# Longformer attention, then a gated MLP, on one core: key and query loads of 80 rows, and another order of the opening

## The chip, the core and the metric

One core of a Trainium2 chip runs the kernel. The time is the device time of one execution in microseconds (us); the times given are medians over runs. TensorE (PE in the profile) does the matmuls and transposes, VectorE (DVE) and ScalarE (ACT) the elementwise work, GpSimd (POOL) small copies and the loads that cast from fp32 to fp16 on their way, SyncE (SP) issues the other transfers. Each engine works through its own instructions in the order of the program; semaphores hold an instruction until what it needs is there.

## The reference

Attention with a band of 32 keys to either side and eight global positions (rows and columns), over 8 batches of 8 heads, 576 positions and 64 channels. Its output, laid out as 4608 tokens of 512 channels, goes through an MLP.

```python
scores = scale * np.matmul(q, k.transpose(0, 1, 3, 2))
mask = np.abs(pos[:, None] - pos[None, :]) <= 32
mask = mask | is_global[:, None] | is_global[None, :]
scores = np.where(mask, scores, -1000000000.0)
...
x = np.matmul(attn, v)            # [8, 8, 576, 64] -> [4608, 512]
h = x @ w_in                      # w_in [512, 2048]
out = (h * np.cos(h)) @ w_out     # w_out [2048, 512]
```

## The kernel before

The 64 heads are handled as 32 pairs; a half-batch is two pairs (four heads). A pair goes through these units, named here as in the string `OPENING`, with the pair's number behind the letter:

- `k`, `q` (`local_k`, `local_q`, for the first ten pairs): sixteen transposes (L598) and sixteen 8-column matmuls that pick the global keys or queries (L319), all into one PSUM bank, which ScalarE or VectorE then copies out (L320, L607, L618, L619; which of the two is told by the strings `ENGINES`). From pair 10 on these are single copies on VectorE from tiles that a transposing DMA has filled (L610, L622).
- `s`: ten score matmuls (L634), exponentials on ScalarE (L637, L641), the mask on VectorE (L638, L642). From pair 10 on L705 to L709.
- `p`: twenty matmuls with the values (L649), then reciprocals and the product `xn` on VectorE (L669).
- `x`: five transposes (L686) and copies into `xT` (L687 to L692); `X` puts in the global rows of a whole batch, on GpSimd (L676).
- `1`: an mlp unit of the first matmul, four 128x512 matmuls (L767) with cosine (L773) and product (L774); it needs the tokens of its tile of 512 in `xT`. `2`: an mlp unit of the second, four matmuls (L805). There are 144 of each. Those that stand in no string are done at the end, alternating.

Other steps issue loads, nearly all from GpSimd's queue: `L` (L284) a half-batch's k and q in natural layout, one row of eight positions to a partition (72 rows, with 3 rows ahead for k and 4 more for q: `KP` is 75, `QP` 76), into `kn`, `qn` or `room`; `M` (L386) its values; `W` (L898) a quarter of `w_in`; `O` (L902) `w_out`; `E` and `A` (L342) gather the global rows; `K` (L271, L275) casts a half-batch from DRAM to DRAM, which `B` brings in on SyncE's queue. `C` (L400) casts the first values on GpSimd, `y` (L406) puts global values in, `I` (L949) loads eight registers on GpSimd. `H` and `g` handle the global rows, `Z` builds masks, `S` spreads global values (L412). `warm` before the string issues dense matmuls on a tile of ones (13, then 4 and 4); `f` (`fill`) would issue a given number of 128x184 matmuls of the same tile into a part of `pv` that nobody reads; it does not occur in the string of before.

The string is worked through step by step, and every step adds its instructions behind those already on each engine. From half-batch 6 on a fixed string per half-batch (`ORDER`) takes over.

```python
nc.gpsimd.dma_start(dst[s % NN][0:n, hs[0] : hs[1]].rearrange("x h r d -> x h (r d)"),
                    dview(src, base - lead * RW * D, (RW * D, n), (S * D, hs[1] - hs[0]), (1, RW * D)))
```

Of the kernel before, what the change touches and what calls it, by code (L numbers as in the profile page):

```python
# [10 lines left out]
FP16 = mybir.dt.float16  # L11
# [6 lines left out]
B, H, S, D = 8, 8, 576, 64  # L18
# [11 lines left out]
RW = 8  # L30
KS = 120
NK5 = 5
KPAD = 3
KP = KPAD + S // RW
QP = S // RW + 4
OFF = (0, 136, 488, 680, 328)
WID = (136, 192, 192, 192, 160)
CA, CB = 488, 384
# [10 lines left out]

SIXTH = "sa 2 2 2 2 sz pa 1 1 2 xa pz G 1 1 2 xz n 1 1 D0 2 kc qc D1 1 kd qd D2 2 1 T"  # L50

OPENING = ("s0 k1 q1 E2 k3 L2 L3 H2 I0 S4 k2 q2 C0.0 q3 C0.1 y0 s1 M1 k4 L4 p0 S5 s2 q4 q5 S2 p1 Z0 M2 s3 "
# [5 lines left out]
ENGINES = ("DAADAAAADD", "DAADADAAAA", "AAAADDDDAD", "AAAAAAAAAA")  # L58
WARM = 13
OK_ALL = float(P * (B * NP * 2 * BP + B))  # L60

# [1 line left out]
def view(ap, *dims):  # L63

    return bass.AP(ap.tensor, ap.offset, [ap.ap[0], *[list(d) for d in dims]])


def dview(ap, offset, *dims):

    return bass.AP(ap.tensor, ap.offset + offset, [list(d) for d in dims])  # L70
# [134 lines left out]
def kernel(  # L205
# [16 lines left out]
    keep = es.enter_context(tc.tile_pool(name="keep", bufs=1))  # L222
# [27 lines left out]
    NN = 4  # L250
    kT = [keep.tile([P, 2, KT], FP16, name=f"kT{i}") for i in range(2)]
    qT = [keep.tile([P, 2, QT], FP16, name=f"qT{i}") for i in range(2)]
    kn = [keep.tile([KP, 2 * 2, RW, D], FP16, name=f"kn{i}") for i in range(2)]
    qn = [keep.tile([QP, 2 * 2, RW, D], FP16, name=f"qn{i}") for i in range(2)]
    vn32 = work.tile([P, 8 * 512], FP32, tag="g", name="vn32")
    room = work.tile([P, NF, TT], FP16, tag="g", name="room")
    w_out16 = const.tile([P, NF, DM], FP16)
    for i in range(2):
        kn.append(room[0:KP, 8 * i : 8 * i + 4].rearrange("p h (r d) -> p h r d", d=D))
        qn.append(room[0:QP, 8 * i + 4 : 8 * i + 8].rearrange("p h (r d) -> p h r d", d=D))  # L260
    vw = [keep.tile([P, NB, 2, D + 1], FP16, name=f"vw{i}") for i in range(NV)]
    NK = 4
    kw = [keep.tile([P, NB, P], FP16, name=f"kw{i}") for i in range(NK)]
# [14 lines left out]
    def load_qk(s, hs=(0, 4)):  # L278

        base = (s * 4 + hs[0]) * S * D  # L280
        for src, dst, n, lead in ((k, kn, KP, KPAD), (q, qn, QP, 0)):
            if s == 0:
                dst, n, lead = [dst[0][lead:]], S // RW, 0
            nc.gpsimd.dma_start(dst[s % NN][0:n, hs[0] : hs[1]].rearrange("x h r d -> x h (r d)"),  # L284
                                dview(src, base - lead * RW * D, (RW * D, n), (S * D, hs[1] - hs[0]), (1, RW * D)))
# [28 lines left out]
    def pick_globals(pr, t, src, ones, n, to):  # L314

        h0 = 2 * (pr % 2)
        for r in range(RW):
            for h in range(2):
                nc.tensor.matmul(t[h * D : (h + 1) * D], src[:n, h0 + h, r], ones[:n, r], start=r == 0, stop=r == RW - 1, skip_group_check=True)  # L319
        COPY[ENGINES[3][pr]](to, view(t, (0, to.shape[1]), (1, G)))  # L320

# [6 lines left out]
    p8 = keep.tile([P, 1], FP32)  # L328
# [169 lines left out]
    def build_mask5():  # L498
# [17 lines left out]
        for t in (0, 1, 4, 2, 3):  # L516
            b0 = D if t == 0 else 0
            n = P if t == 0 else WID[t]
            nc.vector.tensor_scalar(mask5[:, OFF[t] : OFF[t] + n], band5[:, b0 : b0 + n], nk[:, t : t + 1], None, ALU.mult)
        for t in range(NK5):  # L520
            g0 = OFF[t] + (P if t == 0 else D)
            nc.vector.tensor_copy(mask5[:, g0 : g0 + G], view(val[:, t : t + 1], (0, G)))
# [49 lines left out]
    def k5(pr):  # L572
        return kw[pr % NK][:, 0:NK5]

    def q5(pr):
        return qb[pr % NK][:, 0 : 2 * NK5].rearrange("p (n t) c -> p n (t c)", t=2)
# [14 lines left out]
    def turned(src, pr, n):  # L591

        bank = ps.tile([P, 512], FP32, tag="h", bufs=2, name="bank")
        t = view(bank.bitcast(FP16), (QP, RW), (1, QP))
        h0 = 2 * (pr % 2)
        for r in range(RW):
            for h in range(2):
                nc.tensor.transpose(t[h * D : (h + 1) * D, r, 0:n], src[:n, h0 + h, r], ident16[:n, :n])  # L598
        return t, bank[:, 400 : 400 + G]

    def local_k(pr):
        to = kw[pr % NK][:, :, G:]
        if pr < 2 * HY:
            t, g = turned(kn[pr // 2 % NN], pr, KP)
            if pr < PK:
                pick_globals(pr, g, kn[pr // 2 % NN], one_k, KP, k5(pr)[:, :, 0:G])
            COPY[ENGINES[0][pr]](k5(pr)[:, :, G:].rearrange("p n (j r) -> p n j r", r=RW),  # L607
                           view(t, (KS // RW, NK5), (1, KS // RW), (QP, RW)))
        else:
            nc.vector.tensor_copy(to, view(kT[pr // 2 % 2][:, pr % 2], (QB, NB), (1, W)))  # L610

    def local_q(pr):
        to = qb[pr % NK][:, :, G:]
        if pr < 2 * HY:
            t, g = turned(qn[pr // 2 % NN], pr, QP)
            if pr < PK:
                pick_globals(pr, g, qn[pr // 2 % NN], one_q, QP, q5(pr)[:, 1:, 0:G])
            COPY[ENGINES[2][pr]](qb[pr % NK][:, 0, 0:G], t[:, :, 0])  # L618
            COPY[ENGINES[1][pr]](q5(pr)[:, :, G:].rearrange("p n (j r) -> p n j r", r=RW),  # L619
                           view(t[:, :, 1:], (KS // RW, NK5), (1, KS // RW), (QP, RW)))  # L620
# [3 lines left out]
    def scores5(pr):  # L624
# [4 lines left out]
        for t in (0, 1, 4, 2, 3):  # L629
            i, c = (0, OFF[t]) if OFF[t] < CA else (2, OFF[t] - CA)  # L630
            q0 = 0 if t == 0 else P * t - D
# [12 lines left out]
    def values5(pr):  # L644
# [3 lines left out]
        def add(h, t, c0, m, slot, p0, start, stop):  # L648
            nc.tensor.matmul(pv[p0 : p0 + m, h, X * slot : X * slot + X], pm[:, h * CN + OFF[t] + c0 : h * CN + OFF[t] + c0 + m], vp[:, t, h0 + h],  # L649
                             start=start, stop=stop, skip_group_check=True)  # L650
# [254 lines left out]
    with tc.manual_schedule():  # L905
# [6 lines left out]
        for t in (qn[0][64:QP, 2:4], kn[0][0:KPAD, 2:4]):  # L912
            nc.scalar.memzero(t.rearrange("p a b c -> p (a b c)"))
        load_qk(0, (0, 2))
        nc.gpsimd.iota(p_i, pattern=[[0, 1]], base=0, channel_multiplier=1)
        nc.gpsimd.iota(d5_i[:, 0:D], pattern=[[-1, D]], base=56, channel_multiplier=1)
# [3 lines left out]
        nc.gpsimd.affine_select(ident16, ident16, [[-1, P]], ALU.is_equal, 0.0, base=0, channel_multiplier=1)  # L920
        nc.gpsimd.iota(tok_i, pattern=[[1, RW]], base=0, channel_multiplier=RW)
        load_qk(0, (2, 4))
        nc.scalar.memzero(vn_of(0)[0:G, 1:].rearrange("p t d -> p (t d)"))
        nc.scalar.activation(x_sq[:, 0:1], pio2, AF.Exp)
# [3 lines left out]
        build_band()  # L928
        index_rows(1)
        load_qk(1)  # L930
        build_ones()
        build_mask5()
# [67 lines left out]
        outs_by[0] = NTT * NF  # L1000
        for step in OPENING.split():
            if step in "+-":
# [9 lines left out]
        for s in range(6, B * NP // 2):  # L1012
            for step in (SIXTH if s == 6 else ORDER).split():
# [15 lines left out]
                else:  # L1029
                    f, pr = (STEPS | OTHER)[step[0]], 2 * s + "azcd".index(step[1])  # L1030
# [54 lines left out]
```

## Time and profile before

| | |
|---|---|
| median of 3 runs | 356.44 us (356.26 to 356.76) |
| the profiled execution | 355.74 us |
| its span, first to last instruction | 354.0 us |
| mean granted TensorE clock | 0.943 |
| TensorE, VectorE, ScalarE, GpSimd busy | 337.8, 254.3, 223.7, 112.0 us |
| mlp matmuls L767 and L805 | 142.8 and 136.2 us, 381 and 379 ns each |

Of a page or table row: an instruction row gives start, length, engine, line, operation, `out<-in`, shape and count, and in brackets how long its engine had been idle just before and what released it. A stage row gives stretch, length, busy time and number of instructions of each engine, then the granted clock (1.00 is full), the share of the DMA engines and GB/s. A load row gives its size and the time from issue to landing.

### The profile page before, as it was taken

The page shows a single profiled execution, that of the slowest core. Times are in us where ns is not written, and L with a number is a line of the kernel's source. Part 1 is how long each engine was busy: PE and PEld are TensorE (multiplying, and loading weights), DVE is VectorE, ACT ScalarE, POOL GpSimd, SP SyncE. Part 2 cuts the span into 40 slices and gives each one's busy share as a digit, 9 for nine tenths or more (in the row PEclk, how much of TensorE's full clock was granted, in tenths as well). Part 3 has the DMA queues.
Part 4 walks back from the last instruction along what each step waited for, and adds up shares of the span by engine and source line. Part 5 has one row for each costly group of instructions (what it writes and reads, how often), then busy time and mean ns, then how long its engine had stood idle before and what let it go on. Part 6 is the DMA issues. An engine that isn't in the chain of part 4 may idle for free.

```text
span 354.0 us, 8610 instructions
## 1 busy us (share of the span) xinstructions
PE 337.8 (95%) x3294; PEld 177.5 (50%) x3294; DVE 254.3 (72%) x622; ACT 223.7 (63%) x411; POOL 112.0 (32%) x213
## 2 busy tenths in 40 slices
PE   7689999999899999999999999999999999999993
PEld 2468885545454444544444444454545444444442
DVE  6647768959997878787877879797968566556410
ACT  4446657696669685867777676767767756644300
POOL 8665593276802505150705070506000100000000
PEclk9955559999999999999999999999999999999998
DMA  6999999959999999999999999999980000100112
GB/s 105 160 135 81 161 161 200 171 61 149 179 149 118 157 182 144 192 125 185 134 178 142 166 126 206 138 180 142 175 100 32 30 31 30 59 31 31 58 64 68
DMA packets 170708, 43.68 MB, mean 123 GB/s; under 512 B 158468, under 2 KB 165812, under 8 KB 170484
## 3 DMA queue, kind: packets, MB, share of 16 engines
q0 software_dynamic: 73552, 18.64, 58.7%
q1 hardware_dynamic: 96118, 24.17, 48.0%
q8 instruction: 28, 0.46, 0.6%
q10 hardware_dynamic: 990, 0.25, 0.3%
q14 instruction: 20, 0.16, 0.2%
HBM read 44.74 MB, written 19.17 MB: 181 GB/s over the span
## 4 chain that ended last, share of the span: by engine, by line
PE 82%; DMA 7%; ACT 5%; issue 2%; POOL 1%; SPq 1%; DVE 1%; ACTq 0%; POOLq 0%
PE ph L767 32%; PE po L805 32%; DMA qn<-in_q_dram 4%; PE pv L649 3%; DMA kT<-k 3%; PE bank L598 2%; PE tx L750 2%; PE st L705 2%; ACT e L708 2%; PE st L634 2%; PE bank L319 2%; PE pv L725 1%; ACT e L713 1%; PE tx L686 1%; PE po L787 1%
## 5 line engine op out<-in xcount | busy, mean ns | idle before, releaser
L767 PE MATMUL ph<-xT,w_in 128*128 128x512 f16 x576 | 142.8, 381 | 0.8 <-DVE g L774 0.2
L805 PE MATMUL po<-w_out,g 128*128 128x512 f16 x560 | 136.2, 379 | 0.0
L773 ACT ACTIVATE cos<-ph 128x512 f16<-128x512 f32 x144 | 84.4, 597 | 69.7 <-PE ph L767 62.6
L774 DVE TENSOR_TENSOR g<-cos,ph 128x512 f16<-128x512 f16 x144 | 95.9, 684 | 40.9 <-ACT cos L773 39.4
L805 PEld LDWEIGHTS <-g 128*128 128x128 f16 x560 | 53.4, 98 | 63.4 <-issue 0.3
L767 PEld LDWEIGHTS <-w_in 128*128 128x128 f16 x576 | 53.9, 98 | 61.7 <-issue 4.8
L676 POOL COPY xT<-xg 128x4 f16 x64 | 18.9, 295 | 45.3 <-DVE xT L753 38.2
L708 ACT ACTIVATE e<-st 128x512 f16<-128x512 f32 x44 | 23.9, 594 | 11.0 <-PE st L705 10.9
L709 DVE TENSOR_TENSOR pm<-e,mask 128x512 f16<-128x512 f16 x44 | 18.7, 425 | 16.1 <-ACT e L708 14.7
L983 POOL COPY gate<-xn 1x1 f16<-1x1 f16 x8 | 1.4, 181 | 85.4 <-DVE xn L736 85.4
L275 POOL DMA_DIRECT2D q<-in_q_dram x11 | 24.3, 2212 | 0.0
L823 ACT ACTIVATE xn<-xn 128x1536 f16<-128x1536 f16 (+1 forms) x16 | 22.6, 1415 | 0.0
L736 DVE TENSOR_TENSOR xn<-pv,r_all 128x768 f16<-128x768 f32 x22 | 21.1, 958 | 1.0
L812 DVE COPY o<-po 128x512 f32<-128x512 f32 x18 | 12.4, 688 | 8.3 <-PE po L805 8.3
L275 POOL DMA_DIRECT2D k<-in_k_dram x11 | 18.2, 1653 | 0.6 <-issue 0.6
L386 POOL DMA_DIRECT2D vw<-in_v_dram x16 | 15.3, 1102 | 7.6 <-DVE pm L638 4.2
L810 ACT COPY o<-po 128x512 f32<-128x512 f32 x17 | 10.0, 585 | 12.2 <-PE po L805 12.1
L773 ACT ACT_TABLE_LOAD x13 | 16.7, 1283 | 0.2
L637 ACT ACTIVATE e<-st 128x488 f16<-128x488 f32 x20 | 10.5, 578 | 9.1 <-PE st L634 9.0
L610 DVE COPY kw<-kT 128x1320 f16<-128x1320 f16 x22 | 15.3, 694 | 0.1
L708 ACT ACT_TABLE_LOAD x11 | 14.1, 1283 | 0.2
L705 PEld LDWEIGHTS <-kw 64*128 64x128 f16 x484 | 8.3, 95 | 11.0 <-issue 6.8
(182 smaller groups left out, 394.7 us busy)
## 6 DMA issues: line engine op xcount, KB each, us to landing
out_dram<-o SPq DMA_DIRECT2D x35, 256.0 KB
vw<-v SPq DMA_DIRECT2D x32, 165.0 KB
v<-in_v_dram POOLq DMA_DIRECT2D x11, 288.0 KB, 5.4
k<-in_k_dram POOLq DMA_DIRECT2D x11, 288.0 KB, 8.3
q<-in_q_dram POOLq DMA_DIRECT2D x11, 288.0 KB, 11.0
w_in<-in_moe_w_in_dram POOLq DMA_DIRECT2D x4, 512.0 KB, 10.0
w_out<-in_moe_w_out_dram POOLq DMA_DIRECT2D x1, 2048.0 KB, 17.4
vw<-v SPq DMA_DIRECT2D x11, 135.0 KB
```

Of the source, the lines that this page charges most:

```text
L275: nc.gpsimd.dma_start(dst[s].rearrange("t (h d) -> t h d", h=4), dview(src, base, (D, S), (S * D, 4), (1, D)))
L386: nc.gpsimd.dma_start(vn16(s)[G:P, :, h, 0:D], dview(v, ((4 * s + h) * S - 24) * D, (D, KS), (KS * D, NK5), (1, D)))
L676: nc.gpsimd.tensor_copy(xT[:, :, bass.ds(pool_idx[g] + b * S, 1)], xg[:, :, g : g + 1])
L705: nc.tensor.matmul(st[j // 8 * 2 + h][:, j % 8 * C : j % 8 * C + C], kp[hp, j], qp[hp, j], start=True, stop=True)
L708: nc.scalar.activation(e[:, 0:512], st[h], AF.Exp, scale=scale)
L709: nc.vector.tensor_tensor(view(pm[:, h], (1, 512)), e[:, 0:512], view(mask, (1, 512)), ALU.mult)
L736: nc.vector.tensor_tensor(view(xn, (384, 2), (D, 6), (1, D)), view(pv, (512, 2), (65, 6), (1, D)), view(rp, (6, 2), (1, 6), (0, D)), ALU.mult)
L767: nc.tensor.matmul(ph, w_in16[:, j, f * P : (f + 1) * P], xT[:, j, t * TT : (t + 1) * TT], start=(j == 0), stop=(j == NC - 1))
L773: nc.scalar.activation(cos, ph, AF.Sin, bias=pi / 2.0)
L774: nc.vector.tensor_tensor(g, cos, ph, ALU.mult)
L805: nc.tensor.matmul(po, g16[:, f, s * P : (s + 1) * P], w_out16[:, f], start=(f == 0), stop=(f == NF - 1))
L823: nc.scalar.activation(view(xn, (BP * P, 2), (1, n)), view(xn, (BP * P, 2), (1, n)), AF.Square, accum_out=x_sq[:, s : s + 1])
```

## The change

`KQ`, 80, takes the place of `KP` and `QP` as the number of partitions of the tiles and rows that `L` loads for half-batches 1 to 4. The load of half-batch 0 (72 rows, in two halves) and all that reads the tiles are as before: the further rows are loaded and not used. The string `OPENING` and the four strings `ENGINES` are others.

```diff
+KQ = 80
...
-ENGINES = ("DAADAAAADD", "DAADADAAAA", "AAAADDDDAD", "AAAAAAAAAA")
+ENGINES = ("ADDADAAAAA", "AADAADAAAD", "DDADAADAAD", "ADAAAAAAAA")
...
-    kn = [keep.tile([KP, 2 * 2, RW, D], FP16, name=f"kn{i}") for i in range(2)]
-    qn = [keep.tile([QP, 2 * 2, RW, D], FP16, name=f"qn{i}") for i in range(2)]
+    kn = [keep.tile([KQ, 2 * 2, RW, D], FP16, name=f"kn{i}") for i in range(2)]
+    qn = [keep.tile([KQ, 2 * 2, RW, D], FP16, name=f"qn{i}") for i in range(2)]
...
-        for src, dst, n, lead in ((k, kn, KP, KPAD), (q, qn, QP, 0)):
+        for src, dst, n, lead in ((k, kn, KQ, KPAD), (q, qn, KQ, 0)):
```

The start of the old and of the new string:

```diff
-OPENING = ("s0 k1 q1 E2 k3 L2 L3 H2 I0 S4 k2 q2 C0.0 q3 C0.1 y0 s1 M1 k4 L4 p0 S5 s2 q4 q5 S2 p1 Z0 M2 s3 "
-           "S3 + k5 k7 p2 s5 q7 x0 W0 k6 p3 s4 W1 q9 S6 x2 x3 M3 q6 x1 p4 q8 S7 k8 W2 s7 k9 p5 s6 W3 "
-           "X0 O0 1 x4 1 : S8 1 K5 1 p6 M4 1 1 1 S9 n0 x5 1 p7 1 1 x6 1 Z1 E1 1 1 1 1 "
+OPENING = ("E0 q1 E2 k2 s0 q3 W0 k1 H2 q2 I0 L2 f2 L3 Z0 C0.1 C0.0 S7 y0 S2 S4 s1 S3 - M1 k3 p0 k4 s2 q5 "
+           "p1 Z1 s3 f4 L4 S6 k5 x0 q7 x1 q4 k6 M2 p2 S5 s4 W1 k7 p3 s5 q6 M3 k8 x3 p4 s6 k9 x2 + W2 "
+           "q8 O0 p5 X0 s7 q9 p6 s8 1 S9 1 1 1 n0 W3 : x4 p7 1 1 x6 1 + 1 1 S8 1 x5 n2 M4 "
```

The lines of the changed kernel are one higher from L36 on. TensorE between the dense matmuls on ones and s1, before; one row of each unit (here s0, k1, q1, k3 and k2, q2 and q3, y0, s1; `kn_87` and `qn_89` are half-batch 0, `kn_88` and `qn_90` half-batch 1):

```order
L634 MATMUL st<-qb_102,kw_98 128x136
...
L598 MATMUL bank<-ident_70,kn_87 64x75
...
L598 MATMUL bank<-ident_70,qn_89 64x76
...
L598 MATMUL bank<-ident_70,kn_88 64x75
...
L598 MATMUL bank<-ident_70,qn_90 64x76
...
L406 MATMUL rows<-vw_94,one_v 8x256
...
L634 MATMUL st<-qb_103,kw_99 128x136
```

The same place of the change (q1, k2, s0, q3, k1, q2, two fillers, y0, s1):

```order
L599 MATMUL bank<-ident_70,qn_89 64x76
...
L599 MATMUL bank<-ident_70,kn_88 64x75
...
L635 MATMUL st<-qb_102,kw_98 128x136
...
L599 MATMUL bank<-ident_70,qn_90 64x76
...
L599 MATMUL bank<-ident_70,kn_87 64x75
...
L599 MATMUL bank<-ident_70,qn_90 64x76
...
L497 MATMUL pv<-ones_114 128x184
...
L407 MATMUL rows<-vw_94,one_v 8x256
...
L635 MATMUL st<-qb_103,kw_99 128x136
```

s0 and k1 have moved behind units of half-batch 1, one unit (k3) has gone behind s1, and two fillers have come in.

GpSimd from the load of half-batch 1 to the cast of the first values, before:

```order
L284 DMA kn_88<-in_k_dram 75x4x512
L284 DMA qn_90<-in_q_dram 76x4x512
L342 DMA vg_108<-in_v_dram,gidx_rows 128x64 x2
L284 DMA room<-in_k_dram 75x4x512
L284 DMA room<-in_q_dram 76x4x512
...
L951 TENSOR_LOAD gidx_row
L951 ISA x16
L400 CAST vw_94<-vn_91 128x5x2x64 x2
```

and of the change:

```order
L285 DMA kn_88<-in_k_dram 80x4x512
L285 DMA qn_90<-in_q_dram 80x4x512
L343 DMA kg_107<-in_k_dram,gidx_rows 128x64 x2
L343 DMA vg_108<-in_v_dram,gidx_rows 128x64 x2
L899 DMA w_in_133<-in_moe_w_in_dram 128x4x512
...
L952 TENSOR_LOAD gidx_row
L952 ISA x16
L285 DMA room<-in_k_dram 80x4x512
L285 DMA room<-in_q_dram 80x4x512
...
L401 CAST vw_94<-vn_91 128x5x2x64 x2
```

Two gathers and the first quarter of `w_in` have come ahead of the registers, and the loads of half-batches 2 and 3 (`room`) have gone behind them, still ahead of the cast.

VectorE ahead of s10, where the first pairs of the other kind are made (`qb_104`, `kw_100` are pair 10, `qb_105`, `kw_101` pair 11), before:

```order
L967 MEMSET pv 64x2
L622 COPY qb_105<-qT_86 128x11x56
L774 TENSOR_TENSOR g<-cos,ph 128x512
L622 COPY qb_104<-qT_86 128x11x56
...
L610 COPY kw_100<-kT_84 128x11x120
...
L610 COPY kw_101<-kT_84 128x11x120
L709 TENSOR_TENSOR pm<-e,mask 128x512 x2
```

and of the change:

```order
L968 MEMSET pv 64x2
L623 COPY qb_105<-qT_86 128x11x56
L611 COPY kw_100<-kT_84 128x11x120
L611 COPY kw_101<-kT_84 128x11x120
L775 TENSOR_TENSOR g<-cos,ph 128x512 x2
L623 COPY qb_104<-qT_86 128x11x56
L775 TENSOR_TENSOR g<-cos,ph 128x512
L710 TENSOR_TENSOR pm<-e,mask 128x512 x2
```

Both key copies are now ahead of the query copy of pair 10. From s12 on TensorE's rows are the same in both, twelve rows (six fillers and their weight loads) later.

More of the change, by code (lines that the diff above doesn't have):

```diff
@@ L258 @@
     for i in range(2):
-        kn.append(room[0:KP, 8 * i : 8 * i + 4].rearrange("p h (r d) -> p h r d", d=D))
-        qn.append(room[0:QP, 8 * i + 4 : 8 * i + 8].rearrange("p h (r d) -> p h r d", d=D))
+        kn.append(room[0:KQ, 8 * i : 8 * i + 4].rearrange("p h (r d) -> p h r d", d=D))
+        qn.append(room[0:KQ, 8 * i + 4 : 8 * i + 8].rearrange("p h (r d) -> p h r d", d=D))
     vw = [keep.tile([P, NB, 2, D + 1], FP16, name=f"vw{i}") for i in range(NV)]
```

6 rows, old and new, of the table OPENING are left out of this document.

## The prediction

> **What bounds the kernel now.** The page first: span, busy time, and the granted clock in 40 slices of 8.85 us.
>
> ```profile
> span 354.0 us, 8610 instructions
> ...
> PE 337.8 (95%) x3294; PEld 177.5 (50%) x3294; DVE 254.3 (72%) x622; ACT 223.7 (63%) x411; POOL 112.0 (32%) x213
> ...
> PEclk9955559999999999999999999999999999999998
> ```
>
> TensorE is busy for 95% of the span, so the end moves with its work, its holes and its clock. The clock is at half in slices 3 to 6. In the table by stage a mean of 0.77 over 50 to 60 us says that it came back about 54.6 us, after 46% of that stage.
>
> ```profile
> 50.00:60.00 10.00, 10.00 (x86) 5.78 (x83) 8.02 (x21) 6.73 (x13) 6.36 (x6) 0.77 1.22 189
> ```
>
> The same table for two stretches around the fall, one around a hole much later, and the half-clock stretch as a whole (columns: stretch and length, then busy us and count of PE, PEld, DVE, ACT, POOL, then clock, DMA share, GB/s):
>
> ```profile
> 13.60:17.10 3.50, 1.23 (x65) 1.14 (x64) 1.81 (x4) 1.78 (x7) 1.01 (x3) 0.99 1.33 164
> 17.10:20.50 3.40, 1.20 (x37) 1.04 (x38) 0.23 (x1) 0.75 (x2) 2.77 (x4) 0.50 1.02 140
> ...
> 88.70:92.30 3.60, 1.96 (x12) 0.75 (x11) 3.60 (x6) 1.88 (x2) 3.60 (x4) 1.00 1.39 182
> 20.50:52.40 31.90, 31.50 (x636) 26.31 (x633) 21.80 (x67) 19.08 (x52) 20.27 (x30) 0.50 1.38 134
> ```
>
> The clock fell at 17.1 us (0.99, then 0.50). The stretch just before has TensorE busy for 1.23 of 3.50 us (35%); 1.96 of 3.60 us (54%) at 88.7 us did not bring the clock down. The level below which it falls, in these terms, lies between 35% and 54%. Once it is down, 31.50 of 31.90 us of small matmuls do not bring it back; the mlp matmuls behind 52.4 us do. So from 20.5 to 52.4 us **a half-clocked TensorE is the bound**, while VectorE is busy for 21.80 us (68%) and ScalarE for 19.08 us (60%). What made the holes is in TensorE's rows in order of time:
>
> ```profile
> 15.04 0.47 PE L598 MATMUL bank<-ident,kn 75*64 75x75 f16 x16 [1.44 <-DMA kn<-in_k_dram]
> ...
> 18.57 0.17 PE L319 MATMUL bank<-one_k,kn 75*64 75x8 f16 x1 [2.31 <-issue]
> 19.47 0.72 PE L598 MATMUL bank<-ident,qn 76*64 76x76 f16 x16 [0.73 <-DMA qn<-in_q_dram]
> ...
> 21.48 1.23 PE L406 MATMUL rows<-vw,one_v 128*8 128x256 f16 x5
> 22.63 0.91 PE L634 MATMUL st<-qb,kw 64*128 64x136 f16 x10
> ```
>
> A wait for the second keys (1.44 us), one that the profile gives to nothing (2.31 us), one for the second queries (0.73 us). From s1 at 22.63 us on, TensorE has hardly a hole. The next one of size comes at 92 us, where s10 waits behind the copy k10, which took 1.88 us on VectorE:
>
> ```profile
> 92.27 0.50 PE L705 MATMUL st<-qb,kw 64*128 64x64 f16 x22 [1.64 <-POOL kw L582]
> ```
>
> ```profile
> 90.29 1.88 DVE L610 COPY kw<-kT 128x1320 f16<-128x1320 f16 x1
> ```
>
> **The change, part by part.** The 80-row loads first. Two loads of 72 rows, then the two of the second half-batch (75 rows of k, 76 of q), with KB and us from issue to landing; behind them GpSimd's own rows:
>
> ```profile
> kn<-in_k_dram POOLq DMA_DIRECT2D x1, 144.0 KB, 7.8
> qn<-in_q_dram POOLq DMA_DIRECT2D x1, 144.0 KB, 7.9
> ```
>
> ```profile
> qn<-in_q_dram POOLq DMA_DIRECT2D x1, 304.0 KB, 13.1
> kn<-in_k_dram POOLq DMA_DIRECT2D x1, 300.0 KB, 9.4
> ```
>
> ```profile
> 4.93 0.68 POOL L284 DMA_DIRECT2D qn<-in_q_dram  x1
> 5.61 0.69 POOL L284 DMA_DIRECT2D kn<-in_k_dram  x1
> 6.29 1.15 POOL L284 DMA_DIRECT2D qn<-in_q_dram  x1
> 7.74 1.07 POOL L342 DMA_INDIRECT vg<-in_v_dram,gidx_rows  x1 [0.31 <-DVE one_v L503]
> ...
> 10.14 0.82 POOL L284 DMA_DIRECT2D room<-in_k_dram  x1
> ...
> 17.49 1.39 POOL L400 CAST vw<-vn 128x640 f16<-128x640 f32 x2 [2.88 <-issue]
> ```
>
> k landed at 5.61 + 9.4 = 15.0 us, q of nearly the same size, issued 0.68 us later, at 6.29 + 13.1 = 19.4 us, and its issue cost 0.46 us more. In the 72-row pair k and q took the same (7.8 and 7.9 us; q landed at 4.93 + 7.9 = 12.8 us). 76 rows, not the queue, make q late. With 80 rows I let q behave as k does: k itself took 15.0 - 12.8 = 2.2 us behind its forerunner, so q lands about 17 us (bounds: 15.0 with k, 19.4 as now), and three issues ahead of the value cast C0 save 1.4 us.
>
> [...]
>
> Now the order, to s1. The new one runs q1, k2, s0, q3, k1, q2, fill 2, y0, s1; the old one s0, k1, q1, k3, k2, q2, q3, y0, s1. So s0 and k1, which ran before 13 us, are kept back into the stretch that had 1.23 us, and the next has k1, q2 and the fill. GpSimd has two more gathers (about 2.4 us: the old pair started at 7.74 and the load behind it at 10.14), one more w_in issue (some 0.8 us, about what such an issue of a load takes here) and 1.4 us less of issues ahead of C0, which ended at 18.88 us: now about 20.7 us, so y0 can start there (21.48 us before) and s1 comes **about 0.6 us earlier**. k3 has been moved behind s1. Holes remain: ahead of q1, ahead of k2 until 15.0 us, about 16.3 to 17 us, perhaps the 2.31 us again, and ahead of y0. In the stretch from 13.6 us I count k2 0.65, s0 0.5, q3 and k1 up to 0.7: 1.2 to 1.9 us (35 to 54%); in the next one the rest of q3, k1, q2, 0.15 of fill: 1.4 to 2.1 us (41 to 62%). That is inside the gap between the two measured stretches, mostly in its upper half. **I take it that the clock stays up**, narrowly, and price both.
>
> From s1 to the first mlp unit the new order has, besides all that the old one has there, k3, s8, p6 and four fillers. Unit times at half and at full clock, each from a row's start to that of the next:
>
> ```profile
> 28.81 1.56 PE L649 MATMUL pv<-vw,pm 128*128 128x65 f16 x20
> 30.30 0.91 PE L634 MATMUL st<-qb,kw 64*128 64x136 f16 x10
> 31.14 0.72 PE L598 MATMUL bank<-ident,room 75*64 75x75 f16 x16
> ...
> 32.09 0.70 PE L598 MATMUL bank<-ident,room 75*64 75x75 f16 x16
> ...
> 52.38 1.89 PE L767 MATMUL ph<-xT,w_in 128*128 128x512 f16 x4
> 54.07 0.71 PE L686 MATMUL tx<-ident,xn 128*128 128x128 f16 x5
> 54.60 2.76 PE L767 MATMUL ph<-xT,w_in 128*128 128x512 f16 x12
> 57.20 1.03 PE L649 MATMUL pv<-vw,pm 128*128 128x65 f16 x20
> 58.16 2.76 PE L767 MATMUL ph<-xT,w_in 128*128 128x512 f16 x12
> ...
> 71.68 0.55 PE L634 MATMUL st<-qb,kw 64*128 64x136 f16 x10
> 72.16 1.90 PE L805 MATMUL po<-w_out,g 128*128 128x512 f16 x8
> ```
>
> Half clock: p 1.49, s 0.84, k 0.95 us, an mlp unit 1.69 us, a filler 184/512 of a quarter of that, 0.15 us. Full clock: p 0.96, s 0.48, an mlp unit 2.60/3 = 0.87 us. From s12 on both programs have the same matmuls in the same order, so what counts is the time at which that point is reached.
>
> Clock up. TensorE then needs little more than half of its time, and VectorE is next. Its rows:
>
> ```profile
> L638 DVE TENSOR_TENSOR pm<-e,qT 128x488 f16<-128x488 f16 x12 | 4.5, 403 | 0.2 <-ACT e L637 0.2
> L669 DVE TENSOR_TENSOR xn<-pv,r_all 128x640 f16<-128x640 f32 x5 | 4.1, 824 | 0.2
> L642 DVE TENSOR_TENSOR pm<-e,qT 128x768 f16<-128x768 f16 x6 | 3.3, 554 | 1.4 <-ACT e L641 1.4
> ```
>
> ```profile
> 80.00:90.00 10.00, 10.00 (x64) 4.94 (x63) 9.54 (x31) 6.33 (x11) 6.68 (x13) 1.00 2.02 155
> ```
>
> s8 adds 2 x 0.403 + 0.554 = 1.36 us and p6 0.82 plus three small ones of about 0.18, 1.36 us: 21.80 + 2.72 = 24.5 us. How full VectorE can be is bounded by its 68% now and by 95%, the fullest ten us of the opening (80 to 90 us). I take the middle, 82%: 24.5 / 0.82 = 29.9 us, from 20.5 - 0.6 = 19.9 us to 49.8 us. The first mlp unit then starts at 49.8 and not 52.4 us: **-2.6 us** (95%: -6.8; 68%: +3.5, no gain). s8 and p6 are by then done and need not be done later: 0.48 + 0.96, **-1.4 us**. The first mlp unit and x4 are not at half clock: 0.82 + 0.23 (0.53 against 0.30 us by half the work), **-1.05 us**. The wait of s10: VectorE's k10 and TensorE's s10 now have seven mlp units between them (6 us) where three stood (2.6 us), so the 1.64 us go, **-1.6 us**; q10 still has only four, which covers its 0.47 us copy. The fillers lie in holes, 0. W3 behind X0 costs nothing: its chunk is first needed by the 13th mlp unit, over 10 us after its issue, and the loads above landed in 8 to 13 us. Sum: -6.7 us. The profiled execution took 355.74 us (span 354.0 and 1.74 around it), the median of the runs shown is 0.70 us above it: 356.44 - 6.7 = **349.7 us**.
>
> **Rivals.** (1) The clock falls all the same, as for transposes and 8-column picks at 35 to 45% it may. Then k3 0.95, s8 0.84, p6 1.49 and four fillers 0.6 stand on the half-clocked path: +3.9, -0.6 for s1, -1.4 for s8 and p6 done, -1.6 at s10: +0.3, **356.7 us**. For it speak the holes that stay and the 2.31 us that nothing in the diff touches.
>
> [...]
>
> (2) As rival 1, but s10 waits as before, behind q10 or its neighbours, since DVE has k11 ahead of q10 now: 356.7 + 1.6, **358.3 us**, slower. It decides once the q10 copy ends over 3.5 us after it would have been first in line.
>
> (3) The load of 80 rows is no faster than that of 76. The new order has q3 ahead of k1 and q2, so all of these wait for 19.4 us: q3, k1, q2 at half clock 2.85 us, y0 at 22.3, s1 about 0.9 us later than before. +3.9 + 0.9 - 1.4 - 1.6 = +1.8, **358.2 us**, slower. Against it speaks k's own row.
>
> (4) The clock stays up past s1 and falls in a later stretch, halfway: half of the gain, **353.2 us**.
>
> **How the numbers follow.** Forecast 0.45, rival 1 0.20, rival 2 0.13, rival 3 0.12, rival 4 0.10. A measurement can tell 0.2% (0.7 us) from no change. Faster: 0.45 + 0.10 + 0.04 of rival 1 = 0.59; same: 0.12 of rival 1; slower: 0.13 + 0.12 + 0.04 = 0.29. The forecast's own range is 346 (VectorE at 95%, some holes) to 353 us; to hold 8 in 10 the whole must reach to the slower rivals: 346.5 to 358.4 us.
>
> **What would show it.** The clock line: 9 from slice 3 on for the forecast, 5 to about 56 us for rivals 1 to 3. TensorE's row of q3: at 17 us or at 19.4. The q load's issue at 0.7 us and not 1.15. The first mlp unit at 50 or at 56 us. No idle time at s10. The forecast is wrong if the stretch from 13.6 or 17 us has TensorE busy for no more than 40%, or if VectorE, with the clock up, waits for loads instead of working.

## The result, and the profile after

| on one chip | median | ratio to before, 95% interval |
|---|---|---|
| before, 20 runs | 356.93 us (354.60 to 358.25) | |
| the change, 20 runs | 357.07 us (353.95 to 359.82) | 1.0007 [0.999, 1.0024] |

No difference that the measurement can tell: the forecast of 349.7 us did not come, and the time is that of rival 1 (356.7 us), in which the clock falls all the same. The profiled execution of the change took 358.03 us, 0.96 above its median; that of before, 355.74 us, lies 1.19 below the median of its 20 runs. Between these two traces there are thus some 2.1 us that the kernels do not have between them.

The page of the change, the lines that answer to those of before:

```profile
span 356.3 us, 8617 instructions
...
PE 341.6 (96%) x3300; PEld 180.2 (51%) x3300; DVE 254.1 (71%) x623; ACT 224.1 (63%) x410; POOL 110.1 (31%) x213
...
PEclk9755555999999999999999999999999999999999
```

The clock line has its half-clock stretch one slice longer than before. The table by stage of the change, cut where the clock changes (columns as in the prediction's):

```profile
6.57:9.98 3.41, 2.37 (x52) 1.22 (x52) 2.94 (x23) 0.75 (x2) 2.50 (x4) 1.00 1.26 218
9.98:13.39 3.41, 2.13 (x66) 1.32 (x60) 1.82 (x11) 0.84 (x2) 3.00 (x5) 1.00 1.40 183
13.39:61.18 47.79, 43.74 (x814) 34.58 (x815) 31.31 (x90) 27.63 (x71) 26.50 (x39) 0.50 1.51 164
```

The clock is at half for 47.79 us, 14 times 3.41, against 37.5 us before (17.1 to 54.6 us, 11 times 3.41). In all 18 traces the changes of the granted clock lie whole multiples of 3.41 us apart; one such stretch is called a step below, and a window in some of the expectations. The clock did not only fall all the same, it fell one step earlier: the units s0 and k1, which kept TensorE at work up to 13 us before, had been moved out of that stretch. The table of before for its own two steps there:

```profile
10.23:13.65 3.42, 2.94 (x84) 1.94 (x78) 2.98 (x12) 1.90 (x6) 3.11 (x4) 1.00 1.50 144
13.65:17.06 3.41, 1.22 (x63) 1.14 (x64) 1.76 (x4) 1.73 (x7) 0.96 (x3) 1.00 1.32 165
```

The order makes the early fall likely, but it is not the order alone. With s0 and k1 kept back (the change, e2, e3, e6, e8, e15) the clock fell two steps after it came up in all six traces; with them ahead it fell three steps after in seven (before, e1, e5, e7, e9, e11, e16), but two after in e14 and one in e10. e14 is before's own program, and fell at 13.64 us with s0 and k1 in the step, since three of the four dense matmuls on ones that lie in before's step had started ahead of it:

```profile
10.22:13.64 3.42, 2.28 (x77) 1.56 (x75) 2.98 (x12) 1.63 (x4) 3.10 (x4) 1.00 1.54 140
13.64:17.05 3.41, 1.92 (x63) 1.92 (x64) 1.55 (x4) 1.75 (x7) 0.96 (x3) 0.50 1.32 160
```

TensorE's rows of the change in order of time, and the two loads of 80 rows with their issues:

```profile
12.60 0.47 PE L599 MATMUL bank<-ident,qn 76*64 76x76 f16 x16 [1.19 <-ACT qb L620]
...
13.96 0.72 PE L599 MATMUL bank<-ident,kn 75*64 75x75 f16 x16 [0.67 <-DMA kn<-in_k_dram]
...
15.83 0.72 PE L599 MATMUL bank<-ident,qn 76*64 76x76 f16 x16
...
21.72 0.91 PE L635 MATMUL st<-qb,kw 64*128 64x136 f16 x10
...
31.16 0.77 PE L497 MATMUL pv<-ones 128*128 128x184 f16 x4 [0.77 <-DVE xn L670]
...
47.07 1.54 PE L650 MATMUL pv<-vw,pm 128*128 128x65 f16 x20 [1.52 <-issue]
...
57.79 5.28 PE L768 MATMUL ph<-xT,w_in 128*128 128x512 f16 x16
...
94.79 0.49 PE L706 MATMUL st<-qb,kw 64*128 64x64 f16 x22
```

```profile
kn<-in_k_dram POOLq DMA_DIRECT2D x1, 320.0 KB, 8.3
qn<-in_q_dram POOLq DMA_DIRECT2D x1, 320.0 KB, 8.9
```

```profile
5.62 0.68 POOL L285 DMA_DIRECT2D kn<-in_k_dram  x1
6.29 0.65 POOL L285 DMA_DIRECT2D qn<-in_q_dram  x1
```

The 80-row load did what it should: q landed at 6.29 + 8.9 = 15.2 us, its issue took 0.65 and not 1.15 us, q3 runs at 15.83 without a wait, and s1 starts 0.91 us earlier than before (21.72 against 22.63 us). From there to the first mlp unit it is 36.07 us against 29.75: +6.3. Of that k3 is 0.95, s8 0.84 and p6 1.5, the second fillers 0.70 and their own wait 0.77 us (the filler writes `pv`, which VectorE still reads), and a hole in issue ahead of p4 1.52 us. From the first mlp unit to s10 it is 37.00 us against 39.89 (-2.9: s8 and p6 done, the wait of 1.64 us gone), and from s10 to s12 0.3 us less. Sum: -0.9 + 6.3 - 2.9 - 0.3 = +2.2 us at s12; the two executions differ by 2.3 us.

### The profile page after: what moved, and what is told of

Read it like the earlier page. It is cut to its first block, busy times and chain, and to the rows that moved or that the text cites. A ratio compares the mean times of both kernels' runs of the same rounds, so it can differ in the third digit from the quotient of the medians.

```text
span 356.3 us, 8617 instructions
## 1 busy us (share of the span) xinstructions
PE 341.6 (96%) x3300; PEld 180.2 (51%) x3300; DVE 254.1 (71%) x623; ACT 224.1 (63%) x410; POOL 110.1 (31%) x213
## 4 chain that ended last, share of the span: by engine, by line
PE 85%; ACT 5%; issue 3%; POOL 2%; DMA 1%; DVE 1%; POOLq 1%; SPq 0%; ACTq 0%
PE ph L768 34%; PE po L806 33%; PE pv L650 3%; PE tx L751 2%; PE st L706 2%; PE bank L599 2%; ACT e L709 2%; PE st L635 2%; PE pv L726 2%; DMA gidx_col<-in_global_idx_dram 1%; PE bank L320 1%; ACT e L714 1%; PE tx L687 1%; PE po L788 1%; POOLq L952 1%
## 5 line engine op out<-in xcount | busy, mean ns | idle before, releaser
L813 DVE COPY o<-po 128x512 f32<-128x512 f32 x18 | 12.4, 689 | 8.3 <-PE po L806 8.3
L811 ACT COPY o<-po 128x512 f32<-128x512 f32 x17 | 9.9, 585 | 11.4 <-PE po L806 10.8
L387 POOL DMA_DIRECT2D vw<-in_v_dram x16 | 14.2, 889 | 4.4 <-DVE pm L639 1.5
L650 PE MATMUL pv<-vw,pm 128*128 128x65 f16 (+2 forms) x200 | 14.0, 232 | 1.5 <-issue 1.5
L611 DVE COPY kw<-kT 128x1320 f16<-128x1320 f16 x22 | 13.8, 629 | 0.0
```

The costliest lines, as they stand in the source:

```text
L387: nc.gpsimd.dma_start(vn16(s)[G:P, :, h, 0:D], dview(v, ((4 * s + h) * S - 24) * D, (D, KS), (KS * D, NK5), (1, D)))
```

## The experiments

Four sets, each on one chip with its own runs of before (medians: first 361.32, second 356.46, third 361.70, fourth 355.91 us). Times are compared within a set only.

**Parts of the change alone: e1 and e9 (80 rows in the old order).**

```diff
+KQ = 80
```

> The 80-row loads alone, with the old order. Theory A (the half-clocked opening sets the time, the loads only set when its first units start): q of half-batch 1 lands about 3 us earlier, the 0.73 us wait of q2 goes, the clock falls and returns as before: 0.5 to 0.8 us less than before. Theory B (loads and order cancel each other): at least 1.5 us less than before.

> The kernel before with the loads of 80 rows and nothing else. Theory (the early landing of q is worth what TensorE's rows say): s1 about 0.9 us earlier than in before, the clock down and up as in before, the first mlp unit about 0.9 us earlier, and the end 0.5 to 0.9 us earlier, a ratio of 0.9975 to 0.9985. Rival (the earlier start is lost again further on, as idle time behind s10): within 0.2 us of before.

Measured: e1 359.47 us, ratio 0.9949 [0.9931, 0.9967]; e9, on another chip, 359.41 us, 0.9933 [0.9910, 0.9956]. In e9 s1 starts at 21.68 us and the first mlp unit at 50.95, the clock being at half from 15.6 to 53.2 us as in before. The 80 rows are a gain, of 1.9 and 2.3 us on these two chips, more than the 0.5 to 0.9 us expected; at the first mlp unit e9 is 0.9 us ahead of e5 and 1.4 us ahead of before's first trace. The excess stays unexplained: there is no trace of before on these chips. They also showed gaps behind s10 that the other two chips did not have, here in e9:

```profile
90.63 0.50 PE L706 MATMUL st<-qb,kw 64*128 64x64 f16 x22 [1.64 <-POOL kw L583]
...
94.53 0.27 PE L726 MATMUL pv<-vw,pm 128*64 128x65 f16 x4 [0.50 <-issue]
95.24 0.29 PE L726 MATMUL pv<-vw,pm 128*64 128x65 f16 x5 [0.45 <-issue]
96.24 0.26 PE L726 MATMUL pv<-vw,pm 128*64 128x65 f16 x4 [0.71 <-issue]
...
97.10 4.45 PE L768 MATMUL ph<-xT,w_in 128*128 128x512 f16 x12
```

```profile
94.13:97.54 3.41, 1.37 (x17) 0.73 (x18) 0.69 (x1) 0.53 (x2) 1.52 (x2) 1.00 1.52 236
97.54:100.95 3.41, 3.41 (x10) 1.17 (x9) 3.05 (x8) 3.37 (x7) 0.00 (x0) 0.50 1.24 208
```

In e9 the wait and the gaps brought the clock down for one more step: its twelve mlp matmuls took 4.45 us, those at the same place of e1, where the clock stayed, 2.76 us.

**e2 (the new order, loads of 75 and 76 rows).** The change without its `KQ`.

> The new order alone, with loads of 75 and 76 rows. Theory A: q3 waits until about 19.4 us with k1 and q2 behind it, so s1 comes 1 to 2 us later than in the full change: 1 to 2 us more than the change. Theory B: 1.5 us or more above before, too, but made up of later waits (s10, the p units for their values), not of q3 alone. If the load makes no difference: as the change.

Measured: 358.85 us, 0.9918 [0.9890, 0.9945]. The clock is at half from 11.57 to 62.77 us, y0 starts at 22.72, s1 at 23.88 and the first mlp unit at 58.91 us. Against the change's first trace (21.72 and 57.79 us) s1 is 2.2 us and the first mlp unit 1.1 us later, which looks like rival 3 of the prediction. But e3 below, with loads of 80 rows on the same chip, has s1 at the same time:

```profile
23.93 0.91 PE L635 MATMUL st<-qb,kw 64*128 64x136 f16 x10
```

q3 waits 0.75 us in e2 (it starts at 19.00 us, without a wait at 17.75 in e3), but e3's q2 then waits 1.96 us for a copy on ScalarE. Both have gaps of 0.4 to 0.5 us ("issue") among q0's short matmuls from 10 to 13 us, and most of the delay against the change's first trace is there already: s0 starts at 17.34 us in e2, at 16.91 in e3 and at 14.99 in the change. So e2 does not price the slow loads, and the change itself was not run on this chip; what it shows is that the clock falls early with this order whatever the loads.

**e3 and e8 (the change without its fillers).**

```diff
-... I0 L2 f2 L3 ... p1 Z1 s3 f4 L4 ...
+... I0 L2 L3 ... p1 Z1 s3 L4 ...
```

> The change without its two filler steps. Theory A: the four fillers behind s3 took 0.70 us and waited 0.77 us for xn on the half-clocked path, the two ahead of y0 lay in a hole: 1.0 to 1.4 us less than the change, unless the wait only moves on to k5. Rival (the fillers hold the clock a window longer): the clock falls earlier or as early, and the time is the same or longer.

> The change without fillers again, beside the whole change. Theory A: 1.0 to 1.4 us less than the change. Rival (fillers neutral, since the holes they lie in stay): within 0.5 us of the change.

Measured: e3 357.50 us, 0.9902 [0.9875, 0.9929]; e8 356.73 us, 1.0002 [0.9982, 1.0022], beside e6, the change itself, at 357.18 us, 1.0012 [0.9988, 1.0035]. By the medians the fillers cost 0.45 us, which is within the intervals, and not the 1.0 to 1.4 us that I expected: without them the trace of e8 has 0.73 us of issue ahead of p4 in place of 1.33 in e6, and a hole of 0.42 us elsewhere, but q1 waits 2.32 us for its issue, against 1.72. They do not hold the clock: it falls two steps after it came up with them (e6) and without (e8).

**e5 and e6 (before and the change, unchanged, on the second chip).**

> The kernel before, unchanged, beside the others: both theories expect no difference, and the profile shows where the time goes on this chip. Half clock from about 17 to 54.5 us, the first mlp unit near 52 us, 1.64 us of idle time ahead of s10.

> The whole change again, beside its parts. Theory A (a half-clocked opening in both; k3, s8, p6 and the fillers on it cost about what the wait of s10 and the earlier s1 give): within 1 us of before. Rival C (the gain depends on the chip, the parts alone having been 0.5% and 0.8% below before on another one): 2 to 3 us less than before.

Measured: e5 357.05 us, 1.0014 [0.9992, 1.0036]; e6 357.18 us, 1.0012 [0.9988, 1.0035]. The result repeats. In e5 the clock is at half from 17.1 to 54.7 us and s10 waits 1.63 us; in e6 from 12.4 to 60.2 us, and s10 does not wait.

**e7 (s0 and k1 back ahead of q1, p6 and s8 behind the first mlp units, no fillers).**

```diff
-E0 q1 E2 k2 s0 q3 W0 k1 H2 q2 ... q9 p6 s8 1 S9 1 1 1 n0 W3
+s0 k1 E0 q1 E2 k2 q3 W0 H2 q2 ... q9 1 S9 1 1 1 p6 s8 n0 W3
```

> The change without fillers, with s0 and k1 ahead of q1 as in the old order, and with s8 and p6 behind the first four mlp units instead of ahead of them. Theory A: the clock falls a window later, about 17 us instead of 13.4, and s8 and p6 run at full clock: 1 to 1.5 us less than the change without fillers. If the place of the units does not matter: the same as that.

Measured: 358.39 us, 1.0039 [1.0019, 1.0059], 1.7 us over e8 where I expected 1 to 1.5 less. The clock did fall later (15.08 us), but it came back only at 59.45 us, and four mlp units ran at half clock:

```profile
54.66 6.12 PE L768 MATMUL ph<-xT,w_in 128*128 128x512 f16 x16
```

16 matmuls took 6.12 us against the 3.47 us of full clock and the 4.29 us of e8, and behind them s8 and an x unit waited 0.22 and 0.82 us for VectorE and ScalarE. An mlp unit that is brought forward into the half-clock stretch pays for the way back.

**e4 (the clock held by fillers).** More dense matmuls early, and about 95 fillers among the small units, up to p6:

```diff
-E0 q1 E2 k2 s0 q3 W0 k1 H2 q2 I0 L2 f2 L3 ...
+E0 w6 q1 E2 w3 k2 s0 f4 q3 f4 W0 k1 H2 f6 q2 I0 L2 f8 L3 ...
```

> The change with dense matmuls on ones in the early holes (warm 6 and 3, fillers 4 to 8) and ten fillers ahead of each of p1 to p6, about 95 fillers in all instead of 6. If the clock is granted by the share of full-array matmuls in its windows and can be held through the small units: clock at full from about 7 us, the first mlp unit near 50 us instead of 57.8, 4 to 6 us less than before. If it falls all the same: the fillers stand on the half-clocked path at 0.15 to 0.17 us each, 10 us or more above before.

Measured: 359.08 us, 0.9945 [0.9923, 0.9967]; on the same chip e3 took 357.50. The mean clock is 0.967, full from 18.25 to 35.3, from 38.7 to 49.0 and from 59.2 us on, and yet the first mlp unit starts only at 61.92 us. The 96 fillers alone take 11.4 us of TensorE, and one of the s units waits 1.56 us for ScalarE. Two steps of this run, the first and the second after the clock came up:

```profile
4.60:8.01 3.41, 1.58 (x10) 0.56 (x10) 2.25 (x17) 0.93 (x2) 3.10 (x5) 1.00 0.89 135
8.01:11.42 3.41, 2.43 (x54) 1.45 (x55) 1.69 (x14) 0.00 (x0) 2.50 (x4) 1.00 1.41 194
```

The first has TensorE busy for 46% and the clock stayed up; the second for 71%, and it fell. So the busy share does not decide. The first is dense matmuls on ones, the second has transposes of 76 rows and 8-column picks in it.

**e12 (the fillers of e4 as transposes).** My next theory was that transposes do not count.

```diff
-        for _ in range(n):
+        for _ in range(-(-3 * n // 2)):
...
-            nc.tensor.matmul(pv[:, 1, 328:512], ones16, view(ones16, (0, 2), (1, 92)), start=len(filled) == 1, stop=True, skip_group_check=True)
+            nc.tensor.transpose(pv.bitcast(FP16)[:, 1, 656:784], ones16, ident16)
```

> The kernel of e4, in which fillers held the clock up, with every filler a transpose of 128x128 ones and not a matmul of 128x184, three transposes for two matmuls, so that TensorE is busy for about as long. Theory (what holds the clock is matmuls over the whole array, and transposes hardly count): the clock is at half from 13 to 18 us on until the mlp units bring it back, the first mlp unit comes later than in e4 (61.9 us), at 65 us or more, and the time is at least 2 us above e4's. Rival (the busy share of TensorE decides, as the forecast had it): the clock is as in e4, at full for most of 18 to 49 us, and the time within 1 us of e4's against its own before.

Measured: 361.43 us, 0.9994 [0.9959, 1.0029]; mean clock 0.974, first mlp unit at 60.90 us. The theory fell: the clock was held about as in e4. (The time is 2 us worse than e4's against its own before, as the theory had it, but on another chip and not by the clock.) Two steps:

```profile
22.34:25.76 3.42, 3.07 (x90) 2.67 (x85) 2.49 (x7) 1.06 (x5) 3.42 (x5) 1.00 1.37 193
39.41:42.82 3.41, 3.41 (x62) 3.21 (x64) 1.31 (x7) 0.91 (x5) 0.36 (x1) 0.50 1.63 143
```

What ran in the first of them, TensorE's rows:

```profile
22.47 0.39 PE L320 MATMUL bank<-one_k,kn 75*64 75x8 f16 x16
22.79 0.68 PE L497 MATMUL pv<-ident,ones 128*128 128x128 f16 x9
23.82 0.47 PE L599 MATMUL bank<-ident,qn 76*64 76x76 f16 x16 [0.35 <-ACT qb L620]
24.09 0.42 PE L320 MATMUL bank<-one_q,qn 76*64 76x8 f16 x16
24.45 0.84 PE L497 MATMUL pv<-ident,ones 128*128 128x128 f16 x12
25.22 0.72 PE L407 MATMUL rows<-vw,one_v 128*8 128x256 f16 x5
```

Not one matmul over the whole array but the transposes of 128x128, and the clock stays up; in the second step such transposes bring it back from half. What tells them from the small units is the shape: 128*128 weights, the largest of any matmul row here and so taken as the whole array, against 75*64, which is 29% of that. I now count each instruction by **the share of the array that it uses**: columns moved x 0.42 ns (2.60 us for twelve matmuls of 512 columns at full clock; at half clock 0.83 ns, 1.69 us for four) x rows/128 x columns/128, in the step in which it starts. For the step of the rows above: 21 x 128 x 0.42 = 1.13 us; 16 x 76 x 0.42 x 76 x 64 / 16384 = 0.15 us; the picks, y0 and the rest of a k unit 0.1 us: 1.39 of 3.41 us, 0.41. For the step in which the clock of the change fell: four dense matmuls of 512 columns (0.86 us), q1 (0.15) and two lots of picks (0.03), 1.04 of 3.41 us, 0.31.

**e13 (the fillers of e4 on a quarter of the array)** puts this to the test: as many columns moved, 64 rows by 64 columns.

```diff
-nc.tensor.matmul(pv[:, 1, 328:512], ones16, view(ones16, (0, 2), (1, 92)), ...
+nc.tensor.matmul(pv[0:64, 1, 328:512], ones16[0:64, 0:64], view(ones16[0:64], (0, 2), (1, 92)), ...
```

> The kernel of e4, every filler a matmul of 64 rows by 64 columns, a quarter of the array, with the same 184 columns moved, so that TensorE is busy for as long. Theory (what counts is the share of the array in use): the early stretches fall under the level of about 0.35 of the array and the clock is at half from about 11 to 15 us until the mlp units bring it back; the first mlp unit is at 65 us or later (61.9 in e4), and the time at least 2 us above e4's, measured against before on the same chip. Rival (the busy share decides): the clock is as in e4 and e12, at full for most of 18 to 49 us, the first mlp unit at 62 us.

Measured: 367.56 us, 1.0321 [1.0273, 1.0370]; first mlp unit at 67.55 us.

```profile
11.93:15.35 3.42, 3.23 (x81) 1.91 (x79) 1.34 (x6) 0.85 (x2) 1.36 (x4) 1.00 1.18 187
15.35:18.76 3.41, 3.16 (x93) 2.63 (x91) 3.00 (x8) 2.55 (x6) 2.20 (x4) 1.00 0.92 131
18.76:69.96 51.20, 51.20 (x781) 40.95 (x777) 28.18 (x81) 23.26 (x62) 26.33 (x37) 0.50 1.29 144
```

TensorE was busy for 3.16 of 3.41 us (93%) and the clock fell, to stay at half until mlp matmuls came. (It fell at 18.8 us and not at 11 to 15 as I expected: the dense matmuls happened to fill the steps before.) The steps side by side; busy from the tables by stage, the share of the array worked out as above:

```
kernel   step, us        busy   share of the array   clock behind it
before   10.23 - 13.65   86%    0.45                 full
e12      22.34 - 25.76   90%    0.41                 full
e4        4.60 -  8.01   46%    0.38                 full
e4        8.01 - 11.42   71%    0.33                 half
change    9.98 - 13.39   62%    0.31                 half
e13      15.35 - 18.76   93%    0.21                 half
before   13.65 - 17.06   36%    0.09                 half
```

Over the first 75 us of all 18 traces the clock fell behind 22 such steps, with 0.05 to 0.37 of the array in use and TensorE busy for 29 to 93%; all the steps that kept it had 0.34 or more, with TensorE busy for 46 to 100%. The busy shares overlap nearly over their whole range, the shares of the array by 0.03. Behind 75 us the clock fell once before the end of the work, in e9 behind a step of 0.18, and none of the more than 1400 steps that kept it had less than 0.34. That both sides of the shape count is less firm: no run varies rows and columns apart, and in the first 75 us a count by rows/128 alone (fell up to 0.47, kept from 0.36) or by columns/128 alone (0.44, 0.35) overlaps by 0.11 and 0.09. Single steps also move by up to 0.13 with the way in which a matmul over a step's end is counted. To come back from half takes much more: it came back behind 0.66 and up, and steps of up to 0.81 did not do it; where in between it lies stays open.

**e10, e11 and e16 (k10 ahead of q11; with 80 rows too).** The wait of s10 alone, in the old order, and the two gains together:

```diff
-Z5 q11 1 q10 g13 1 k10 1 K7
+Z5 k10 q11 1 q10 g13 1 1 K7
```

> The kernel before with the copy k10 on VectorE ahead of the two copies of q10 and q11, nothing else. Theory (the wait of s10 is time on the path): the 1.64 us of idle time ahead of s10 go, no other idle time of TensorE comes in for them, and the end is 1.4 to 1.6 us earlier, a ratio of 0.9955 to 0.996. Rival (the wait was cover for something else: TensorE then waits for its instructions or for the copy of q10): 0 to 0.5 us.

> The kernel before with the loads of 80 rows and k10 ahead of q10 and q11; the old order otherwise. Theory (two terms that add): 2.0 to 2.5 us faster than before, a ratio of 0.993 to 0.9945, and so faster than the change as well. Rival (one term eats the other, since an earlier s10 finds k10 or q10 later): no more than 1.6 us.

> The old order with loads of 80 rows and k10 ahead of q10 and q11, beside before and the change on one chip. Theory (the terms add, and the old order keeps the clock longer): 2.0 to 2.5 us under before where before takes 356.5 us, about 5 us where it takes 361; 2 us or more under the change in both cases. Rival: within 1 us of the change.

Measured: e10 357.78 us, 0.9892 [0.9864, 0.9920]; e11 356.38, 0.9847 [0.9816, 0.9879]; both on the third chip; in e10 the clock fell one step after it came up (0.35 of the array), came back behind the next (0.80) and fell again at 17.6 us. e16, the same kernel as e11 on the fourth, 354.44, 0.9946 [0.9923, 0.9969], beside the change (e15) at 357.20. In e10, e11 and e16 s10 no longer waits, but some of it comes back further on, at s12:

```profile
103.84 1.02 PE L768 MATMUL ph<-xT,w_in 128*128 128x512 f16 x4 [0.62 <-DVE g L775]
105.81 0.71 PE L706 MATMUL st<-qb,kw 64*128 64x64 f16 x22 [0.94 <-issue]
```

From s10 to s12 e16 takes 16.5 us where before took 14.6: of about 3 us that s10 comes earlier, 1.1 us are left at s12 against before's first trace and 1.35 against e14's. e16 is nevertheless the version that beats both, by 2.8 us against the change and 1.5 against before on the fourth chip. On the third the gains are larger (3.9 us for k10 alone); e9 there has the wait, the gaps behind it and the step at half clock that follows, 1.64 + 2.35 + 1.7 us; e10 has none of these, but waits of 0.59, 0.49 and 0.94 us further on. That before loses the same there would explain its 361.7 us, but no trace of it was taken on that chip.

**e14 and e15 (before and the change on the fourth chip).**

> The kernel before, unchanged, for a profile on the chip of these runs. Theory: clock at half from 17 to 55 us, first mlp unit at 51 to 52.4 us, s10 waits 1.6 us. If the chip is one of those on which before takes 361 us, the profile shows what it loses there: by the theory single matmuls with gaps of 0.5 us behind s10, over 2 us, as in e1 and e9; rival: somewhere else.

> The change, unchanged, beside before. Theory (rival 1 of the prediction, the clock falls all the same): within 1 us of before where before takes about 356.5 us. Where before takes about 361 us, the change has no wait at s10 and so none of what follows it: 2 to 3 us faster there.

Measured: e14 357.58 us (one run; the 23 others of before there have a median of 355.91); e15 357.20 us, 1.0022 [0.9996, 1.0049]. e14 shows no gaps behind s10, so the question of the slower chips stays open. Its clock fell at 13.64 us and not at 17, as shown above, and its first mlp unit starts at 53.30 us, later than the 51 to 52.4 us expected. The profiled execution of e15 was its fastest, 352.62 us, and shows what the change is worth when the clock comes back early:

```profile
10.93:14.34 3.41, 1.17 (x48) 0.89 (x48) 1.59 (x9) 0.99 (x2) 2.07 (x4) 1.00 1.27 189
14.34:45.06 30.72, 28.41 (x607) 23.64 (x599) 21.91 (x58) 16.95 (x48) 18.60 (x23) 0.50 1.56 159
45.06:48.47 3.41, 3.41 (x55) 2.77 (x54) 2.11 (x9) 1.91 (x5) 0.00 (x0) 0.50 1.21 190
48.47:54.06 5.59, 5.17 (x155) 4.21 (x150) 4.95 (x16) 4.54 (x14) 2.46 (x9) 1.00 1.24 207
```

The step to 48.47 us happened to hold an x, a p and an s unit and most of k8's transposes (0.16, 0.22, 0.21 and 0.07 of the array, 0.66 in all, at 0.83 ns per column), and the clock came back ahead of the first mlp unit, which starts at 54.06 us. Two of the 12 runs were of this kind (352.62 and 353.43 us, mean clock 0.948 and 0.947; the others 0.931 to 0.938), and in the first comparison one of 20 (353.95 us, 0.951).

The half-clock stretches of the change, 47.79 and 30.72 + 3.41 us, are 14 and 10 steps, and the same program fell at 12.4, 13.4 and 14.3 us in its three traces (e6, the first trace, e15). These lie about 1 us apart and not a whole step, so in these traces the steps were not in line with the first instruction of the span.

## Why the prediction was wrong, point by point

- **The failing step: "I take it that the clock stays up", narrowly.** It rested on a level between 35% and 54% of TensorE's busy time, from two stretches. Busy time was the wrong measure in these runs (93% fell in e13, 46% held in e4): the stretch with 54% held large mlp matmuls, and the new order's stretches hold transposes of 75 rows and 8-column picks. In shares of the array the units I counted there, k2, s0, q3 and k1, come to 0.16 + 0.37 + 0.16 + 0.16 us (s0 moves 1744 columns over half of the array), about 0.25 of a step: by the level that the runs show, the clock would have fallen there even had it arrived at full. It did not arrive: the step before, 0.31 without s0 and k1, brought it down already. The prediction moved these two units into its stretch and did not ask what was left of the one that they came from. The clock was then at half to 61.2 us, and the first mlp unit started at 57.8 us where the forecast had 49.8.
- **Rival 1's transposes.** Rival 1 had the clock fall for transposes and 8-column picks. It fell, but that they are transposes was not shown to be the reason: in e12 transposes of 128x128 held the clock (1.00 over 22.34 to 25.76 us, 0.41 of the array) and brought it back (0.50 up to 42.82 us, full behind it). Small shapes counted little, transposes or not: behind a step with matmuls of 64 rows by 64 columns, 0.21 of the array, the clock fell in e13.
- **The load of 80 rows: right, and larger.** q landed at 15.2 us where I took 17; s1 came 0.91 us earlier where I took 0.6. e1 and e9 confirm it alone. The q load took 8.9 us for 320 KB in 80 rows (9.3 us in e1) against 13.1 us for 304 KB in 76, so rival 3, a load no faster than that of 76 rows, did not come. That q in 80 rows would go as k does in 75 was an estimate from k's row; why 76 rows take longer, no run shows.
- **The wait of s10: right.** s10 starts without one in the change, and e10 shows the same with k10 moved alone. That all of its 1.6 us reach the end was too much: in e16 part comes back at s12.
- **VectorE as the next bound at full clock: not refuted.** In e15's stretch at full clock TensorE is busy for 92% and VectorE for 4.95 of 5.59 us, 89%, between the 82% that I took and the 95% of its bound. From the k8 row to the first mlp unit it took 6.03 us there, 8.41 at half clock in the change's trace. What no run had is the full clock at a profit: e4 and e12 held it for most of the opening with 11 us of fillers, and e4 took 1.6 us more than e3 on the same chip. (At VectorE's bound of 95% the prediction's terms give -6.7 us, not -6.8.)
- **Fillers at nothing: wrong.** They do not lie in holes only: the second lot waits 0.77 us for VectorE and takes 0.70 us. The run without them was 0.45 us faster, which is less than that sum and within the noise.
- **Rival 1's sum held by its terms:** +3.9 for k3, s8, p6 and the fillers, -0.6, -1.4 and -1.6: 356.7 against 357.07 us measured. It lacked the holes of 0.77 and 1.52 us and the first mlp units at half clock (16 matmuls of which 3.4 us ran so), and had the gain of the loads too small; these cancel, so it is in part luck that the sum comes within 0.4 us of the median.

## What to carry to other kernels

Before a forecast rests on the clock, count for each step (3.41 us here) what share of the array (128*128 here) the instructions use, not how long TensorE is busy: here it fell below about 0.35, and came back only above about 0.66. Small transposes and thin matmuls stayed at half clock here though TensorE was busy for all of many steps (31.50 of 31.90 us in before, 51.20 of 51.20 in e13), so a gain is to be sought in fewer of them or in what they wait for. And a unit that is moved out of a stretch is missing there: ask what it held up.

## What the runs showed that I had not expected

- The clock went by the part of the array in use and not by TensorE's busy time: 93% busy with shapes of a quarter to a third of the array fell (e13); 46% busy, mostly with the whole of it, held (e4).
- One program has executions 5 us apart on one chip (the change, 352.62 to 357.77 us), the fastest of them where a 3.41 us step happened to lie well.
- The four chips differ: before took 355.91 and 356.46 us on two, 361.32 and 361.70 on the others, and on these two six of eight traces have chains of gaps of about 0.5 us ("issue") between short matmuls, behind s10 (e1, e9) or from 10 to 13 us (e2, e3, e4, e12). No trace of the other two chips has such a chain.
- Holes in issue of 0.6 to 2.65 us ahead of a short matmul come and go with the order of the instructions. The 2.31 us of before, which the prediction took to be touched by nothing in the diff, is in all eight traces of the old order and in none of the new. No run was made on them, but the traces hold a lead, loads of instructions, 16 KB each, on a DMA queue of their own: all 17 holes of 0.6 us or more between 14 and 60 us end 1.3 to 1.8 us behind the end of such a load (before: load from 15.74 to 16.91 us, hole to 18.57; the change: load from 44.60 to 45.53, hole ahead of p4 to 47.07). Most of the seven or so such loads of a trace in that time have no hole behind them, and the holes ahead of q1 (2.32 us in e8) and of s12 (0.94 us) have no such load ahead, so the cause stays open.
